# Token numbers written behind the gate's value, and the rank product moved to other banks and later steps

## The chip, the core and the metric

The kernel runs on one core of a Trainium2 chip. The metric is the device time in microseconds (us) of one execution. Instructions run on TensorE (PE: matmuls; its weight loads are listed as PEld), VectorE (DVE), ScalarE (ACT) and GpSimd (POOL); SyncE (SP) and POOL issue DMAs. Each engine takes its instructions in the order in which they were queued to it, and an instruction that waits for a semaphore holds up what is queued behind it.

## The reference

Three stages follow each other. A gated delta-rule attention over 4 batches, 8 heads, 768 tokens and a head size of 48, then a dense layer pair, then a layer with 8 experts of which each token takes one:

```python
for t in range(S):
    kt, vt, bt = (k_n[:, :, t], v[:, :, t], beta[:, :, t, None])
    y[:, :, t] = np.einsum('bhd,bhde->bhe', q[:, :, t], state)
    v_old = np.einsum('bhde,bhd->bhe', state, kt)
    state = state + bt[:, :, :, None] * np.einsum('bhd,bhe->bhde', kt, vt - v_old)
...
h = x @ w_in                      # 384 -> 2048
x = np.maximum(0.01 * h, h) @ w_out
...
e_idx = np.argmax(x @ w_gate, axis=1)          # one of 8 experts
out[mask] = gate_w[mask, None] * eom[mask, e, None] * (np.maximum(x[mask] @ w1[e], 0.0) @ w2[e])
```

## The kernel before

**Chunks and steps.** The 768 positions are cut into 12 chunks of 64 (`NCH`); with the 4 batches a chunk is 256 tokens. The function `weave` runs a loop over n from 0 to 95. Chunk p = n // 8 is in its attention while n runs over its eight steps s = n % 8 (generator `chain`), and beside it run the dense layer of the chunk before (`moe1_up`, `moe1_down`, a sixteenth of its width in two halves at each step) and the tail of the chunk before that (`moe1_tail`, `gate`, `place`). For each pair of chunks the generator `prepare` makes key grams (`k_gram`), norms and the inverse of a 32x32 triangular matrix (`inverse`), which for all pairs but the first is a row of 60 small operations on POOL (L207 and L209) that ends with L211. `back` converts the expert weights (L476 on ACT, L477 on DVE) in the gaps.

**The tail of a chunk.** `moe1_tail` reads the dense layer's result from PSUM into two tiles `row` of 128 tokens, 386 words wide: 384 words of values (L535 on ACT, L536 on DVE), then at word 384 the gate's value (L627) and at word 385 the token number (L628, a constant plus an offset; it needs nothing but the buffer). Three steps later the gate product runs (`gate`, at s = 4), and two steps after that `place` runs (s = 6): five matmuls make `rk`, the rank of each token among those of its expert (L604 to L608), DVE turns it into positions `pi` (L619 to L625), and POOL scatters both row tiles into the DRAM table `xd` by an indirect DMA each (L630). A row tile's buffer is used again two chunks later, so a chunk's first write into it waits until the scatter of the chunk two before has been read out.

**What sets the order.** On PE the order from n = 16 on is the order in which the program is written (a manual schedule). On DVE, ACT, POOL and SP a scheduler places each instruction by its own model of when inputs and buffers are ready, unless `issue_after` ties it to another one. PSUM banks come from pools: `psL` (2 banks; `h` of `moe1_up`, the gate product, and `rk`), `psS` (2 banks; key grams `ga`, query grams `gq`, the outputs `y`), `psA` (2 banks; `ks` of the chain), `psO`.

**Lines that the steps touch.** L317 on DVE writes the start value of a chunk's `ks`; L325 on PE adds the old state's product to it and is the chunk's first matmul of the chain; L295 splits `ks` into `r` and `u` for the matmuls L302. L493 is `moe1_up`'s matmul, L498 to L501 make its activation, L512 is `moe1_down`'s matmul. L260 to L262 mask and split the query gram. L164 is the first POOL operation of a pair's norms, L218 turns the inverse for the chain.

Of the kernel before, what the change touches and what calls it, by code (L numbers as in the profile page):

```python
# [8 lines left out]
F32 = mybir.dt.float32  # L9
# [3 lines left out]
ALU = mybir.AluOpType  # L13
# [5 lines left out]
CH = 64  # L19
NCH = S // CH  # L20
# [494 lines left out]
def flip_pe(k, dst, src, engines, n):  # L515
    for h in range(2):
        tp = k.psS.tile([128, 3, 128], F32, tag="psS", name=f"tp{h}_{n}")
        for kk in range(3):
            q = 3 * h + kk
            k.nc.tensor.matmul(tp[:, kk], src[:, 128 * q : 128 * q + 128], k.ident, start=True, stop=True)  # L520
        d = dst[:, 3 * h : 3 * h + 3]
        if engines[h] is k.nc.scalar:
            engines[h].activation(d, tp, AF.Copy)
        else:
            engines[h].tensor_copy(d, tp)


def moe1_tail(k, c, o):
    nc = k.nc
    V, A, G, PE = nc.vector, nc.scalar, nc.gpsimd, nc.tensor  # L530
    row, rv = [], []
    for t in range(2):
        row.append((k.m2 if c >= NCH - 2 else k.p2).tile([128, XCOL], I32, tag="row" if c >= NCH - 2 else f"row{c % 2}", name=f"row{t}{c}"))
        rv.append(row[t][:, 0:384].bitcast(F16))
        A.activation(rv[t][:, 0:384], o[t], AF.Copy, scale=2.0**-14)  # L535
        V.scalar_tensor_tensor(rv[t][:, 384:768], o[t], 2.0**-14, rv[t][:, 0:384], op0=ALU.mult, op1=ALU.subtract)  # L536
    xT2 = [k.m2.tile([128, 6, 128], F16, tag="x2t", name=f"x2t{t}{c}") for t in range(2)]
    if c < NCH - 2:
        for t in range(2):
            nc.sync.dma_start_transpose(out=xT2[t], in_=rv[t])  # L540
        yield
        yield
        yield
    else:
        yield
        for t in range(2):
            flip_pe(k, xT2[t], rv[t], (A, A), f"{t}{c}")
            yield
    lg_ps = k.psL.tile([128, 2, 16], F32, tag="psL", name=f"lgp{c}")
    for t in range(2):  # L550
        n = 0
        for kk in range(3):
            for l, r in PASSES:
                PE.matmul(lg_ps[:, t], xT2[t][:, 3 * l + kk], k.wg[r][:, kk], start=(n == 0), stop=(n == 8))
                n += 1
    fin = gate(k, c, lg_ps, row)
    yield
    if c < NCH - 2:
        yield
    fin()  # L560
    yield


def gate(k, c, lg_ps, row):
    nc = k.nc
    V, A, G, PE = nc.vector, nc.scalar, nc.gpsimd, nc.tensor

    def small(n, shape, dt=F32):
        return k.m1.tile(shape, dt, tag=f"g_{n}", name=f"g_{n}{c}")

    def bc(ap, n=8):
        return ap.unsqueeze(2).to_broadcast([128, 2, n])

    lg = small("lg", [128, 2, 16])
    V.tensor_scalar(lg, lg_ps, 2.0**-18, None, op0=ALU.mult)
    mx = small("mx", [128, 2])
    V.tensor_reduce(mx, lg[:, :, 0:8], axis=AX.X, op=ALU.max)
    ls = small("ls", [128, 2, 8])
    V.tensor_tensor(ls, lg[:, :, 0:8], bc(mx), op=ALU.subtract)
    ex = small("ex", [128, 2, 8])  # L580
    A.activation(ex, ls, AF.Exp)
    s = small("s", [128, 2])
    V.tensor_reduce(s, ex, axis=AX.X, op=ALU.add)
    eq = small("eq", [128, 2, 8])
    i8 = k.iota8.unsqueeze(1).to_broadcast([128, 2, 8])
    V.scalar_tensor_tensor(eq, ls, 0.0, i8, op0=ALU.is_ge, op1=ALU.mult)
    ix = small("ix", [128, 2])
    V.tensor_reduce(ix, eq, axis=AX.X, op=ALU.min)
    oh = small("oh", [128, 2, 8])
    V.tensor_tensor(oh, i8, bc(ix), op=ALU.is_equal)  # L590
    ohh = small("ohh", [128, 2, 8], F16)
    V.tensor_copy(ohh, oh)
    return lambda: place(k, c, row, lg, s, oh, ohh)


def place(k, c, row, lg, s, oh, ohh):
    nc = k.nc
    V, A, G, PE = nc.vector, nc.scalar, nc.gpsimd, nc.tensor

    def small(n, shape, dt=F32):  # L600
        return k.m1.tile(shape, dt, tag=f"g_{n}", name=f"g_{n}{c}")

    rk = k.psL.tile([128, 3, 8], F32, tag="psL", name=f"rk{c}")
    PE.matmul(rk[:, 0], k.tri, ohh[:, 0], start=True, stop=True)  # L604
    PE.matmul(rk[:, 1], k.tri, ohh[:, 1], start=True, stop=False)
    PE.matmul(rk[:, 1], k.ones, ohh[:, 0], start=False, stop=True)
    PE.matmul(rk[:, 2], k.ones, ohh[:, 0], start=True, stop=False)
    PE.matmul(rk[:, 2], k.ones, ohh[:, 1], start=False, stop=True)  # L608
    ol = small("ol", [128, 2, 8])
    og = small("og", [128, 2])  # L610
    V.tensor_tensor(ol, oh, lg[:, :, 8:16], op=ALU.mult)
    V.tensor_reduce(og, ol, axis=AX.X, op=ALU.add)
    z = small("z", [128, 2])
    A.activation(z, og, AF.Exp, scale=-1.0)
    V.tensor_scalar(z, z, 1.0, None, op0=ALU.add)
    V.scalar_tensor_tensor(z, s, 1e-9, z, op0=ALU.add, op1=ALU.mult)
    V.reciprocal(z, z)
    pos = small("pos", [128, 2, 8])
    V.tensor_tensor(pos, rk[:, 0:2], k.run.unsqueeze(1).to_broadcast([128, 2, 8]), op=ALU.add)  # L619
    V.tensor_tensor(k.run, rk[:, 2], k.run, op=ALU.add)  # L620
    V.tensor_tensor(pos, pos, oh, op=ALU.mult)
    ps = small("ps", [128, 2])
    V.tensor_reduce(ps, pos, axis=AX.X, op=ALU.add)
    pi = k.m2.tile([128, 2], I32, tag="pi", name=f"pi{c}")
    V.tensor_copy(pi, ps)  # L625
    for t in range(2):
        V.tensor_scalar(row[t][:, 384:385].bitcast(F32), z[:, t : t + 1], 2.0**-27, None, op0=ALU.mult)  # L627
        V.tensor_scalar(row[t][:, 385:386], k.tid[:, t : t + 1], float(CH * c), None, op0=ALU.add)  # L628
    for t in range(2):
        nc.gpsimd.indirect_dma_start(  # L630
            out=k.xd[:, :], out_offset=bass.IndirectOffsetOnAxis(ap=pi[:, t : t + 1], axis=0), in_=row[t][:, :], in_offset=None
        )
# [260 lines left out]
def weave(k):  # L893
# [130 lines left out]
    for n in range(8 * NCH):  # L1024
# [42 lines left out]
        if down is not None:  # L1067
            moe1_down(k, *down)
            if down[1] == 7:
                tail = moe1_tail(k, down[0], k.o)  # L1070
# [27 lines left out]
def finish(k, up, tail):  # L1098
    ts = None
    for s in range(9):  # L1100
        down, up = up, None
        if s < 8:
            moe1_up(k, NCH - 1, s)
            up = (NCH - 1, s, k.gg)
        if s == 0:
            ts = [gather(k, i, k.ridx0) for i in range(4)]
        if tail is not None:
            next(tail, None)
        moe1_down(k, *down)
        if down[1] == 7:  # L1110
            tail = moe1_tail(k, down[0], k.o)
    next(tail)
    moe2_up(k, ts[0])
    next(tail)
    next(tail)
    moe2_up(k, ts[1])
    next(tail)
    moe2_down(k, ts[0])
    next(tail)
    moe2_up(k, ts[2])  # L1120
    moe2_down(k, ts[1])
    moe2_up(k, ts[3])
    moe2_down(k, ts[2])
    moe2_tables(k)
    ahead = {s: gather(k, s, k.ridx) for s in range(4)}
    moe2_down(k, ts[3])
    return ahead
# [121 lines left out]
```

## Time and profile before

| what | value |
|---|---|
| median of 3 runs | 967.54 us (966.23 to 970.23) |
| profiled execution, own time | 970.8 us |
| its span | 969.1 us |
| PE busy | 778.9 us, 80% of the span |
| PEld busy | 599.7 us, 62% |
| DVE busy | 588.6 us, 61% |
| ACT busy | 405.0 us, 42% |
| POOL busy | 348.6 us, 36% |
| mean granted TensorE clock | 0.948 of full speed |

The table is an average over stages. From 0 to about 200 us the attention starts and weights are converted; from 200 to about 610 us the weave runs with `prepare` beside it; from there to 745 us it runs without it; then come the experts. A time in brackets at the end of a trace row is how long the engine stood idle before that row, followed by what ended it.

### The profile page before, as it was taken

How to read it: one execution, taken by the hardware profiler on the slowest of the kernel's cores; microseconds unless marked ns; L12 is line 12 of the kernel's file. 1: busy time of each engine (PE TensorE's matmuls, PEld its weight loads, DVE VectorE, ACT ScalarE, POOL GpSimd, SP SyncE). 2: the span in 40 equal slices, each digit the busy share in tenths (PEclk: the TensorE clock that was granted, in tenths of full speed). 3: DMA queues.
4: the chain of work that ended last, by engine and by line, in shares of the span. 5: the costliest groups of instructions: out<-in, count | busy, mean ns of one | idle time of the engine just before them, and what ended most of it. 6: DMA issues, size and time to landing. Idle time of an engine off the chain costs nothing. (4 is left out here: it accounts for less than half of the span.)

```text
span 969.1 us, 36443 instructions
## 1 busy us (share of the span) xinstructions
PE 778.9 (80%) x15996; PEld 599.7 (62%) x15996; DVE 588.6 (61%) x1304; ACT 405.0 (42%) x788; POOL 348.6 (36%) x526
## 2 busy tenths in 40 slices
PE   3033796858978698768978688999989889999994
PEld 3023565646756476646756466777767778877782
DVE  6999995747868577766958468686546222222221
ACT  5247655534664356634564245555332111111110
POOL 0027993684028810585028800000202322122210
PEclk9999997988999799998999789999999999999998
DMA  8425332435544455544554344555681743899460
GB/s 267 150 81 175 131 111 61 131 103 157 163 129 139 142 162 157 131 134 138 162 146 126 103 109 148 137 155 127 257 353 37 232 84 76 197 317 300 104 172 11
DMA packets 100965, 145.67 MB, mean 150 GB/s; under 512 B 43120, under 2 KB 70547, under 8 KB 97986
## 3 DMA queue, kind: packets, MB, share of 16 engines
q1 hardware_dynamic: 95682, 128.29, 44.9%
q0 software_dynamic: 5120, 15.00, 4.8%
q8 instruction: 127, 2.08, 0.9%
q14 instruction: 36, 0.29, 0.1%
HBM read 152.28 MB, written 35.42 MB: 194 GB/s over the span
## 5 line engine op out<-in xcount | busy, mean ns | idle before, releaser
L493 PE MATMUL h<-xx,win 128*128 128x256 f16 x1728 | 223.4, 287 | 4.8 <-issue 3.2
L493 PEld LDWEIGHTS <-win 128*128 128x128 f16 x1728 | 172.0, 103 | 37.5 <-issue 5.0
L512 PE MATMUL o<-wout,gh 128*128 128x384 f16 x768 | 188.0, 330 | 2.2 <-ACT gh L500 0.9
L835 PEld LDWEIGHTS <-wb 128*128 128x128 f16 x2016 | 118.5, 99 | 10.7 <-issue 4.2
L512 PE MATMUL o<-wout,gl 128*128 128x384 f16 x384 | 124.2, 329 | 0.0
L500 ACT ACTIVATE gh<-h 128x512 f16<-128x512 f32 x96 | 57.3, 597 | 159.5 <-DVE h L499 159.5
L630 POOL DMA_INDIRECT xd<-row,pi x24 | 25.3, 1055 | 261.2 <-issue 139.2
L839 DVE SCALAR_TENSOR_TENSOR h<-hp,h 128x512 f16<-128x512 f32 x48 | 33.2, 691 | 126.0 <-ACT h L838 126.0
L835 PE MATMUL hp<-xT,wb 128*128 128x128 f16 x1728 | 103.5, 223 | 5.0 <-DMA xT<-row 2.5
L512 PEld LDWEIGHTS <-gh 128*128 128x128 f16 x768 | 73.8, 99 | 44.7 <-issue 3.7
L838 ACT ACTIVATE h<-hp 128x512 f16<-128x512 f32 x48 | 28.7, 597 | 166.1 <-PE hp L835 166.1
L849 PE MATMUL o<-wb,h 128*128 128x384 f16 x576 | 97.4, 326 | 0.0
L501 DVE TENSOR_TENSOR gl<-h,gh 128x512 f16<-128x512 f32 x96 | 66.3, 690 | 46.0 <-ACT gh L500 45.9
L209 POOL TENSOR_TENSOR x<-x,tmp 128x30 f32<-128x30 f32 (+9 forms) x150 | 86.0, 573 | 11.1
L499 DVE SCALAR_TENSOR_TENSOR h<-h,g 128x512 f32<-128x512 f32 x96 | 66.4, 691 | 37.6 <-ACT g L498 37.5
L207 POOL TENSOR_TENSOR tmp<-x 128x30 f32<-128x30 f32 (+9 forms) x150 | 84.8, 565 | 10.8
L498 ACT ACTIVATE g<-h 128x512 f32<-128x512 f32 x96 | 57.4, 598 | 69.5 <-PE h L493 64.9
L853 POOL DMA_INDIRECT out_dram<-y,row x24 | 23.9, 998 | 150.0 <-DVE y L852 133.8
L849 PEld LDWEIGHTS <-h 128*128 128x128 f16 x576 | 55.3, 98 | 34.3
L477 DVE SCALAR_TENSOR_TENSOR whl<-we,whl 128x512 f16<-128x512 f32 x96 | 73.7, 779 | 0.0
L302 PE MATMUL ks<-r,z 32*32 32x48 f16 x2304 | 27.2, 189 | 44.0 <-ACT z L235 27.1
L476 ACT ACTIVATE whl<-we 128x512 f16<-128x512 f32 x96 | 57.9, 623 | 0.1
(250 smaller groups left out, 1132.5 us busy)
## 6 DMA issues: line engine op xcount, KB each, us to landing
wb<-wd SPq DMA_DIRECT2D x56, 1536.0 KB
we<-in_we_dram SPq DMA_DIRECT2D x96, 256.0 KB
wd<-whl SPq DMA_DIRECT2D x96, 256.0 KB
kt<-in_kt_dram SPq DMA_DIRECT2D x22, 224.0 KB
qt<-in_qt_dram SPq DMA_DIRECT2D x22, 224.0 KB
nv<-in_kv_dram SPq DMA_DIRECT2D x12, 384.0 KB
kn<-in_kv_dram SPq DMA_DIRECT2D x12, 384.0 KB
w<-in_win_dram SPq DMA_DIRECT2D x6, 512.0 KB
```

The lines of the kernel that those rows point to most:

```text
L207: E.tensor_tensor(tv, x[:, q, j : j + 1].to_broadcast([128, n, j]), x[:, j : j + 1, 0:j].to_broadcast([128, n, j]), op=ALU.mult)
L209: k.after = E.tensor_tensor(x[:, q, 0:j], x[:, q, 0:j], tv, op=ALU.add)
L476: nc.scalar.activation(hl[:, 0], w32, AF.Copy, scale=sc)
L477: nc.vector.scalar_tensor_tensor(hl[:, 1], w32, sc, hl[:, 0], op0=ALU.mult, op1=ALU.subtract)
L493: PE.matmul(hp[:, ff], k.win[l][:, f, kk], xx[:, r, kk], start=(n == 0), stop=(n == 8))
L498: A.activation(g32, hp, AF.Copy, scale=0.01 * 2.0**-10)
L499: V.scalar_tensor_tensor(hp, hp, 2.0**-10, g32, op0=ALU.mult, op1=ALU.max)
L500: k.mark = A.activation(gh, hp, AF.Copy)
L501: k.mark_gl = V.tensor_tensor(gl, hp, gh, op=ALU.subtract)
L512: k.mark_down = k.nc.tensor.matmul(k.o[t], gg[l][:, ff, 128 * t : 128 * t + 128], k.wout[r][:, f], start=(f == 0 and i == 0), stop=(f == N ...
L835: PE.matmul(hp[:, ff], w1[:, l, kk, 128 * f : 128 * f + 128], t.xT[:, 3 * r + kk], start=(i == 0), stop=(i == 8))
L849: nc.tensor.matmul(o, t.h[l][:, f], w2[:, r, f], start=(i == 0), stop=(i == 23))
```

## The change

The write of the token number (L628, now L631) is tied by `issue_after` to the write of the gate's value into the same row tile. `rk` comes from the banks of `psS` instead of `psL` for chunks 0 to 9. And for chunks 0 to 8 the loop in the tail pauses three times instead of once, so that `place` runs four steps after the gate instead of two: at s = 0 of the next chunk instead of s = 6.

```diff
@@ moe1_tail
     if c < NCH - 2:
-        yield
+        for _ in range(3 if c < NCH - 3 else 1):
+            yield
     fin()
@@ place
-    rk = k.psL.tile([128, 3, 8], F32, tag="psL", name=f"rk{c}")
+    ps = (k.psS, "psS") if c < NCH - 2 else (k.psL, "psL")
+    rk = ps[0].tile([128, 3, 8], F32, tag=ps[1], name=f"rk{c}")
...
-        V.tensor_scalar(row[t][:, 384:385].bitcast(F32), z[:, t : t + 1], 2.0**-27, None, op0=ALU.mult)
-        V.tensor_scalar(row[t][:, 385:386], k.tid[:, t : t + 1], float(CH * c), None, op0=ALU.add)
+        last = V.tensor_scalar(row[t][:, 384:385].bitcast(F32), z[:, t : t + 1], 2.0**-27, None, op0=ALU.mult)
+        with k.tc.issue_after(last.ins):
+            V.tensor_scalar(row[t][:, 385:386], k.tid[:, t : t + 1], float(CH * c), None, op0=ALU.add)
```

DVE before, at the start of chunk 3 (n = 24). `row02` is the row tile of chunk 2's first 128 tokens; its buffer is that of `row00`, chunk 0's:

```order
L260 TENSOR_TENSOR gq3_1_4387<-gq3_1_4387,amask_119 128x512
L628 TENSOR_SCALAR row02_6373<-crow_528 128x1
L262 TENSOR_TENSOR ap3_4300<-gq3_0_4386,ap3_4300 128x512
L262 TENSOR_TENSOR ap3_4300<-gq3_1_4387,ap3_4300 128x512
L317 SCALAR_TENSOR_TENSOR ks03_4547<-nv3_2064,nw1_907 128x384
L317 SCALAR_TENSOR_TENSOR ks13_4548<-nv3_2064,nw1_907 128x384
```

The same place of DVE now, up to the positions of chunk 0 (`pi0`):

```order
L260 TENSOR_TENSOR gq3_1_4358<-gq3_1_4358,amask_119 128x512
L262 TENSOR_TENSOR ap3_4300<-gq3_0_4357,ap3_4300 128x512
L262 TENSOR_TENSOR ap3_4300<-gq3_1_4358,ap3_4300 128x512
L317 SCALAR_TENSOR_TENSOR ks03_4518<-nv3_2064,nw1_907 128x384
...
L295 SCALAR_TENSOR_TENSOR r3_4515<-ks13_4519,r3_4515 128x384
L621 TENSOR_TENSOR g_pos0_4702<-rk0_4687,run_530 128x16
L622 TENSOR_TENSOR run_530<-rk0_4687,run_530 128x8
L623 TENSOR_TENSOR g_pos0_4702<-g_pos0_4702,g_oh0_4128 128x16
L499 SCALAR_TENSOR_TENSOR h2_0_4661<-h2_0_4661,g322_0_4680 128x512
L625 TENSOR_REDUCE g_ps0_4706<-g_pos0_4702 128x2
L627 CAST pi0_4708<-g_ps0_4706 128x2
```

The early write into chunk 2's row tile is gone from between L260 and L262, and the five small operations on chunk 0's ranks, which stood ahead of L260, now stand behind L317 and L295.

POOL at the end of a pair's inverse (L211; L164 is the first operation of the next pair), the difference between the two, with the scatters of chunk 0 (`row00`, `row10`) and chunk 1:

```order
 L209 TENSOR_TENSOR x2_3523<-x2_3523,tmp2_3699 128x30
 L211 TENSOR_TENSOR x2_3523<-x2_3523,nz2_3527 128x1024
-L630 DMA xd_57<-row01_4868,pi1_5696 24577x386
-L630 DMA xd_57<-row11_4871,pi1_5696 24577x386
+L633 DMA xd_57<-row00_3496,pi0_4708 24577x386
+L633 DMA xd_57<-row10_3499,pi0_4708 24577x386
+L633 DMA xd_57<-row01_4868,pi1_6111 24577x386
+L633 DMA xd_57<-row11_4871,pi1_6111 24577x386
 L164 TENSOR_TENSOR nz3_6404<-ny3_6403 128x32
```

Chunk 0's two scatters, which stood inside the inverse, have moved behind it; chunk 1's stay where they were. The same holds for chunks 2 and 3, 4 and 5, 6 and 7.

## Rows read from the trace of the kernel before

**Rows 1.** Busy time by stretch: length, then PE, PEld, DVE, ACT, POOL, clock, DMA.

```profile
200.00:610.00 410.00, 333.13 (x8188) 249.73 (x8187) 283.10 (x579) 207.01 (x413) 181.71 (x303) 0.91 0.48 138
```

**Rows 2.** Waits from 200 to 610 us: us in total, times, longest.

```profile
PE ks L325 <- DVE ks L317: 46.1, 16, 11.2
PE rk L604 <- DVE gl L501: 6.2, 4, 2.2
...
DVE row L628 <- DMA xd<-row,pi: 44.7, 8, 11.5
```

**Rows 3.** Timeline of DVE, start of chunk 3: start, length, line.

```profile
218.62 0.15 DVE L628 TENSOR_SCALAR row<-crow 128x1 int32<-128x1 f32 x1 [11.52 <-DMA xd<-row,pi]
...
219.89 1.59 DVE L317 SCALAR_TENSOR_TENSOR ks<-nv,nw 128x384 f32<-128x384 f32 x2
...
225.35 1.01 DVE L295 SCALAR_TENSOR_TENSOR r<-ks,r 128x384 f16<-128x384 f32 x2
...
227.40 0.70 DVE L499 SCALAR_TENSOR_TENSOR h<-h,g 128x512 f32<-128x512 f32 x1 [1.04 <-ACT g L498]
```

**Rows 4.** Timeline of POOL, end of the same pair's inverse.

```profile
215.65 1.19 POOL L630 DMA_INDIRECT xd<-row,pi  x1 [0.24 <-issue]
...
228.95 1.91 POOL L211 TENSOR_TENSOR x<-x,nz 128x1024 f32<-128x1024 f32 x1
```

**Rows 5.** Timeline of PE, start of chunk 3.

```profile
220.73 0.20 PE L325 MATMUL ks<-sc,kc 48*64 48x48 f16 x1 [11.16 <-DVE ks L317]
221.53 1.48 PE L325 MATMUL ks<-sc,kc 48*64 48x48 f16 x95 [0.61 <-DVE ks L317]
222.95 3.73 PE L493 MATMUL h<-xx,win 128*128 128x256 f16 x18
```

**Rows 6.** Timeline of DVE and PE, starts of chunks 5, 7 and 9.

```profile
327.29 0.15 DVE L628 TENSOR_SCALAR row<-crow 128x1 int32<-128x1 f32 x1 [8.06 <-DMA xd<-row,pi]
...
437.83 0.15 DVE L628 TENSOR_SCALAR row<-crow 128x1 int32<-128x1 f32 x1 [9.69 <-DMA xd<-row,pi]
...
547.57 0.15 DVE L628 TENSOR_SCALAR row<-crow 128x1 int32<-128x1 f32 x1 [9.76 <-DMA xd<-row,pi]
...
549.65 0.19 PE L325 MATMUL ks<-sc,kc 48*64 48x48 f16 x1 [7.74 <-DVE ks L317]
```

**Rows 7.** Timeline of DVE and PE, start of chunk 4.

```profile
267.46 0.15 DVE L628 TENSOR_SCALAR row<-crow 128x1 int32<-128x1 f32 x1 [1.27 <-DMA xd<-row,pi]
...
268.14 0.18 PE L325 MATMUL ks<-sc,kc 48*64 48x48 f16 x1 [0.93 <-DVE ks L317]
268.61 1.01 PE L325 MATMUL ks<-sc,kc 48*64 48x48 f16 x95 [0.29 <-DVE ks L317]
269.55 2.14 PE L493 MATMUL h<-xx,win 128*128 128x256 f16 x18
```

**Rows 8.** Busy time by stretch behind the first long wait, columns as above.

```profile
220.70:226.50 5.80, 5.16 (x114) 4.08 (x114) 4.84 (x7) 2.82 (x5) 5.17 (x9) 0.52 0.56 161
```

**Rows 9.** Timeline of DVE and POOL, scatters of chunk 1 and next norms.

```profile
262.89 0.15 DVE L625 CAST pi<-g_ps 128x2 int32<-128x2 f32 x1
...
268.19 1.19 POOL L630 DMA_INDIRECT xd<-row,pi  x1 [3.39 <-DMA xd<-row,pi]
...
276.98 0.68 DVE L499 SCALAR_TENSOR_TENSOR h<-h,g 128x512 f32<-128x512 f32 x1
...
286.03 0.23 POOL L164 TENSOR_TENSOR nz<-ny 128x32 f32<-128x32 f32 x1 [16.65 <-DVE ny L162]
```

**Rows 10.** Timeline of DVE and ACT, next users of inverse and row.

```profile
257.74 1.24 DVE L218 STREAM_TRANSPOSE zt<-x 128x1024 f32<-128x1024 f32 x1
...
278.71 0.86 ACT L535 ACTIVATE row<-o 128x384 f16<-128x384 f32 x2
```

**Rows 11.** Timeline of DVE, two L477 beside L211, and two without.

```profile
229.79 2.22 DVE L477 SCALAR_TENSOR_TENSOR whl<-we,whl 128x512 f16<-128x512 f32 x2
...
342.61 1.28 DVE L477 SCALAR_TENSOR_TENSOR whl<-we,whl 128x512 f16<-128x512 f32 x2
```

## The prediction

> **What bounds the kernel now.** I read the busy table by stretch first. From 200 to 610 us PE is busy for 333.13 of 410 us and DVE for 283.10 [rows 1]: no engine is full, PE is nearest, so what makes PE wait there is worth reading. The waits of that stretch, longest in total first, then show one line far ahead of all others. PE stood 46.1 us before L325 for DVE's L317, and 6.2 us before L604; DVE itself stood 44.7 us, in 8 places, before L628 for a scatter to be read out [rows 2]. The timelines show that these are one thing. At the start of chunk 3 DVE has everything for L262 and L317, but L628 stands ahead of them and waits 11.52 us [rows 3]. L628 writes a constant into the row tile of chunk 2, into which L535 writes its first values only at 278.71 [rows 10]; it needs the buffer of chunk 0, whose scatter POOL issues at 215.65, in between the operations of an inverse that ends at 230.86 [rows 4]. L317 follows at 219.89, and PE, out of work until then, starts L325 at 220.73 after 11.16 us [rows 5]. The starts of chunks 5, 7 and 9 show the same, with 8.06, 9.69 and 9.76 us [rows 6]; those of chunks 4, 6, 8 and 10 show it small, 1.27 us at the first of the four [rows 7].
>
> **Part 1, the token number behind the gate's value.** The write itself is kept, 0.15 us on DVE, and is now where the buffer has long been this chunk's own, since L535 and L536 have written to it. Nothing waits there. What goes is the stall, and I ask at each place what is late next. Chunk 3: without L628, L262 starts 11.5 us earlier, and so does L317, which is 2.1 us ahead of PE's L325 by the distance of 218.62 and 220.73; PE then meets its data at 209.2 to 209.6, when it is ready. All of its 11.16 us go. Chunks 5 and 7: DVE gains 8.06 and 9.69. Chunk 9: PE stood only 7.74 us [rows 6], since it came later than DVE; 7.74 go. Together 11.16 + 8.06 + 9.69 + 7.74 = 36.65 us. Small places: DVE's waits leave 44.7 - (11.52 + 8.06 + 9.69 + 9.76) = 5.67 us for the four, 1.42 each; PE stood 0.93 before L325 at the one shown [rows 7]. So 0.93 to 1.42 at each, 3.7 to 5.7 us in all; I take the middle, 4.7.
>
> **The clock behind a stall.** Behind the 11.16 us the granted clock is 0.52 for 5.8 us, the lower of its two levels (1.2 of 2.4 GHz) [rows 8]: the 95 matmuls of L325 take 1.48 us and the 18 of L493 3.73 [rows 5], where chunk 4's start shows 1.01 and 2.14 [rows 7]. That is 0.47 + 1.59 = 2.06 us, and 8.2 us if the three other long stalls cost as much. The Trainium skill (TensorE: Matmul & The Clock Gate, HAM oscillation) says that idle gaps throttle PE again, so that the matmuls behind each run cold; rows 8 agree, and by that rule alone the whole 8.2 would come back. I take half, 4.1, because DVE is late next there: L295, which feeds PE's next matmuls of the chain, ends at 226.36, 7.7 us after L628 [rows 3], and this stretch of DVE's queue does not shorten with PE's clock. Bounds 0 and 8.2.
>
> **Part 2, the rank product in other banks and two steps later.** The five matmuls and five small DVE operations stay; they move. In psL, `rk` took a bank that L501 had still to read, and four times PE waited, 6.2 us in all [rows 2]. In psS the banks of the query grams have been read by L262 ahead of L317, so at the new place, behind L493 of the next chunk's first step, nothing has to be waited for. The 6.2 us don't all come back: `moe1_down`, a few matmuls behind, needs the same L501. Bounds 0 and 6.2; I take half, 3.1. On DVE the first three small operations now stand between L295 and L499. At chunk 3's start L499 stood 1.04 us for ACT [rows 3], which covers them; at chunk 4's start L499 has no wait before it at 276.98 [rows 9], so there they can cost their own time, some 0.5 us if each takes what L628 and L625 take, 0.15 us [rows 3, 9]. Four such places, 2 us at most; I take 0, as PE has the whole of `moe1_down` before it needs L499's result.
>
> **Part 3, what the later positions do to POOL.** The scatters of the even chunks leave the inverse and stand behind it. The inverse gets shorter by them (1.19 us for the one shown [rows 4]). Two users could be late. The first is the row tile's next writer, L535, at 278.71 [rows 10], some 13 us earlier now, near 265; chunk 0's two scatters would start near 228, when the inverse ends. The one issued at 215.65 was read out by 218.62, 3.0 us later [rows 3, 4]; two behind each other make 6 us, 10 with some delay, so 238. Cover: 265 - 238, some 27 us. The second is the inverse's user L218 at 257.74 [rows 10], near 244 now, against an end near 228: 16 us of cover. The odd chunks' scatters are tighter. Before, `pi` was cast at 262.89 and the second scatter ended at 269.38, 6.5 us later; L164, held by DVE, started at 286.03 [rows 9]. Now the cast stands behind the L499 that ran at 276.98, so near 278.0, the second scatter ends near 284.5, and 1.5 us of cover are left. If the scatter takes 4 us longer, POOL is 2.5 us late at each of three pairs, and DVE's norms behind it, 7.5 us in all. I take 0.
>
> **The sum.** 36.65 + 4.7 + 4.1 + 3.1 = 48.6 us off the profiled execution's own 970.8 us (its span of 969.1 and 1.7 around it) gives 922.2. That execution stands 3.3 us above the median of 967.54; against the median the same gain gives 919.0, which I forecast. Gains at their upper bounds: 36.65 + 5.7 + 8.2 + 6.2 = 56.8, so 910.8. At their lower bounds, 36.65 + 3.7 = 40.4, less 2 and 7.5 of costs, 30.9 are left, so 936.7.
>
> **Rivals.**
>
> *POOL and DVE get in each other's way, 930.* The 39 us in which DVE stood were time in which POOL had the tiles to itself. Beside POOL's L211 two L477 took 2.22 us, without it 1.28 [rows 4, 11]. If the three long operations of each of four inverses now each meet a DVE that has no slack, that is 12 x 0.94 = 11.3 us, so 930.3. Against it: such meetings exist before too, and move rather than multiply. The Trainium skill (SBUF — State Buffer, Who interferes with whom) says that a DVE instruction with two SBUF inputs and a POOL one that reads SBUF lock each other out whole. L477 has two such inputs, and the rows agree in direction: 2.22 against 1.28 is a delay of half of L211's 1.91, not of all of it; by the rule in full it would be 12 x 1.91 = 22.9 us, so 942.
>
> *The wait moves on to DVE, 943.* If DVE's queue behind the stall had been what PE would meet next everywhere, half of the gain is given back within the chunk: 967.5 - 24.3 = 943.2. Against it: DVE's 283.10 us in a stretch of 361 would be 78%, PE's 333.13 would be 92%, so PE is still nearer to full.
>
> *The change doesn't reach the stall, 967.5.* It would need an early write to stay ahead of L317. The order of DVE's instructions shows none, so this has little chance.
>
> *Slower.* L535 takes L628's part: it waits for the same scatter, now behind the whole inverse, and holds ACT's queue, with DVE's L536 behind it. It decides from 27 us on: if the scatters land more than that later than I reckon, each of the seven chunks that use a row buffer again waits for the rest. To eat 48.6 us, each has to be late by 27 + 7 us. At 10 us beyond the cover the time is 967.5 - 48.6 + 70 = 989. Against it: the 27 us count from the end of the inverse, behind which POOL's queue holds nothing but the scatters and L164.
>
> **Chances.** The forecast (909 to 926) 0.72, POOL and DVE in each other's way (926 to 936) 0.14, the wait on DVE 0.07, no change 0.04, slower 0.03. The range 909 to 934 takes in the first and most of the second, about 0.83. A measurement of this kernel can tell about 0.5%, 5 us, from no change: faster 0.93, the same 0.04, slower 0.03.
>
> **What would show it.** In the profile after: no wait of DVE for a scatter between 200 and 610 us, and PE before L325 under 1 us at each chunk's start; the clock at its upper level behind it; L493 near 2.1 us there; the starts of chunks 3 and 5 some 96.5 us apart (108.67 before, by 218.62 and 327.29 [rows 3, 6], less a quarter of 48.6). PE before the rank product: nothing. POOL's L164 still released by DVE; if by a scatter, part 3 was wrong. A wait of ACT's L535 for a scatter would make the whole prediction wrong, and so would PE waiting as long for L295 or L499 as it did for L317.

## The result and the profile after

The changed kernel took 918.89 us (median of 4 executions, 910.93 to 920.65) beside 968.88 us for the kernel before: a ratio of 0.9463, 95% interval 0.9432 to 0.9495. The forecast was 919.0. In a second comparison, beside its variants, the ratio was 0.9518 (0.9495 to 0.9541), 924.46 against 971.97 us; there the gain is 4.8% and not 5.4%. Both lie in the forecast's range when they are put on its base of 967.54 us: 915.6 and 920.9. That the total came so near is partly luck, as the terms below show.

The profiled execution took 919.24 us (span 917.4), 51.6 us less than the 970.8 of before. The same stretch of the kernel now runs from 200 to about 566 us. Its busy times, in the columns of [rows 1]:

```profile
200.00:566.00 366.00, 330.17 (x8228) 246.49 (x8227) 291.27 (x585) 210.15 (x419) 189.62 (x302) 0.96 0.56 157
```

PE is busy for 330 of 366 us, 90% against 81% before. The granted clock is 0.96 of full speed against 0.91. DVE's busy time in this stretch rose from 283 to 291 us.

PE's waits there (us in total, times, longest), which answer to [rows 2]. No line of DVE waits for `xd<-row,pi` any more; its longest wait for anything but ACT is now 2.0 us:

```profile
PE ks L302 <- issue: 9.8, 5, 2.6
PE ks L325 <- DVE ks L317: 6.4, 10, 1.5
PE rk L606 <- DVE lx L142: 5.6, 2, 3.1
PE ks L325 <- issue: 4.2, 1, 4.2
```

The 46.1 us before L325 have become 6.4. The 6.2 us before the rank product have become 5.6 with another name: not L501, the reader of `psL`'s banks, but L142, a reader of key grams in `psS`. The two rows that end in "issue" stand for gaps in the middle of a run of equal matmuls, for which the profile shows no releaser.

The start of chunk 3 on DVE and then on PE (start, length; in brackets the idle time ahead), against [rows 3, 5]:

```profile
204.74 1.29 DVE L262 TENSOR_TENSOR ap<-gq,ap 128x512 f16<-128x512 f32 x2
205.95 1.50 DVE L317 SCALAR_TENSOR_TENSOR ks<-nv,nw 128x384 f32<-128x384 f32 x2
```

```profile
206.58 0.18 PE L325 MATMUL ks<-sc,kc 48*64 48x48 f16 x1 [0.20 <-DVE ks L317]
207.50 0.95 PE L325 MATMUL ks<-sc,kc 48*64 48x48 f16 x95 [0.74 <-DVE ks L317]
208.38 2.14 PE L493 MATMUL h<-xx,win 128*128 128x256 f16 x18
210.36 0.17 PE L606 MATMUL rk<-g_ohh,cmat 128*128 128x8 f16 x1
```

L317 follows L262 with nothing between. PE waits 0.20 us where it waited 11.16, and behind it the 18 matmuls of L493 take 2.14 us instead of 3.73. The rank product of chunk 0 stands behind them, without a wait.

At the start of chunk 4 it is otherwise, and this is what the prediction missed:

```profile
260.37 0.17 PE L606 MATMUL rk<-g_ohh,cmat 128*128 128x8 f16 x1 [2.54 <-DVE lx L142]
263.61 0.97 PE L104 MATMUL ga<-kc 48*64 48x64 f16 x95 [0.86 <-DVE run L622]
```

With chunk 4 `prepare` begins the next pair. Its key grams `ga` have just been put into both banks of `psS`. The rank product has to wait until L142 has read one of them, and the next key gram then waits for L622, the rank product's own reader. Chunk 8 shows 3.06 us in the same place. At chunk 6 key grams lie in both banks too, but there the rank product comes behind a gap of 4.22 us in PE's work and has nothing left to wait for.

POOL at that place, the scatters of chunk 1 and the norms of the next pair, against [rows 9]:

```profile
265.26 0.96 POOL L633 DMA_INDIRECT xd<-row,pi  x1 [30.33 <-ACT gh L500]
268.65 0.96 POOL L633 DMA_INDIRECT xd<-row,pi  x1 [2.43 <-DMA xd<-row,pi]
273.43 0.23 POOL L164 TENSOR_TENSOR nz<-ny 128x32 f32<-128x32 f32 x1 [3.82 <-DVE ny L162]
```

The second scatter ends at 269.61, and POOL then idles for 3.82 us until DVE has its input: the norms are still released by DVE.

### The profile page after: what moved, and what is told of

Read it like the earlier page. It is cut to its first block, busy times and chain, and to the rows that moved or that the text cites. A ratio compares the mean times of both kernels' runs of the same rounds, so it can differ in the third digit from the quotient of the medians.

```text
span 917.4 us, 36446 instructions
## 1 busy us (share of the span) xinstructions
PE 768.7 (84%) x15996; PEld 590.7 (64%) x15996; DVE 592.6 (65%) x1304; ACT 405.2 (44%) x788; POOL 356.6 (39%) x526
## 3 DMA queue, kind: packets, MB, share of 16 engines
q1 hardware_dynamic: 95682, 128.29, 47.4%
## 5 line engine op out<-in xcount | busy, mean ns | idle before, releaser
L493 PE MATMUL h<-xx,win 128*128 128x256 f16 x1728 | 218.6, 284 | 3.3 <-issue 1.7
L493 PEld LDWEIGHTS <-win 128*128 128x128 f16 x1728 | 169.6, 101 | 33.2 <-issue 3.6
L512 PE MATMUL o<-wout,gh 128*128 128x384 f16 x768 | 188.2, 330 | 3.2 <-DVE row L536 1.8
L512 PE MATMUL o<-wout,gl 128*128 128x384 f16 x384 | 124.4, 329 | 0.4 <-DVE gl L501 0.2
L838 PEld LDWEIGHTS <-wb 128*128 128x128 f16 x2016 | 116.5, 98 | 11.4 <-issue 7.8
L838 PE MATMUL hp<-xT,wb 128*128 128x128 f16 x1728 | 101.5, 220 | 5.8 <-DMA xT<-row 5.8
L512 PEld LDWEIGHTS <-gh 128*128 128x128 f16 x768 | 73.1, 99 | 45.5 <-issue 4.5
L501 DVE TENSOR_TENSOR gl<-h,gh 128x512 f16<-128x512 f32 x96 | 66.3, 690 | 44.8 <-ACT gh L500 44.5
L209 POOL TENSOR_TENSOR x<-x,tmp 128x30 f32<-128x30 f32 (+9 forms) x150 | 90.5, 604 | 11.3
L477 DVE SCALAR_TENSOR_TENSOR whl<-we,whl 128x512 f16<-128x512 f32 x96 | 72.6, 768 | 0.0
L302 PE MATMUL ks<-r,z 32*32 32x48 f16 x2304 | 27.7, 188 | 46.7 <-ACT z L235 27.1
```

The costliest lines, as they stand in the source:

```text
L209: k.after = E.tensor_tensor(x[:, q, 0:j], x[:, q, 0:j], tv, op=ALU.add)
L477: nc.vector.scalar_tensor_tensor(hl[:, 1], w32, sc, hl[:, 0], op0=ALU.mult, op1=ALU.subtract)
L493: PE.matmul(hp[:, ff], k.win[l][:, f, kk], xx[:, r, kk], start=(n == 0), stop=(n == 8))
L501: k.mark_gl = V.tensor_tensor(gl, hp, gh, op=ALU.subtract)
L512: k.mark_down = k.nc.tensor.matmul(k.o[t], gg[l][:, ff, 128 * t : 128 * t + 128], k.wout[r][:, f], start=(f == 0 and i == 0), stop=(f == N ...
L838: PE.matmul(hp[:, ff], w1[:, l, kk, 128 * f : 128 * f + 128], t.xT[:, 3 * r + kk], start=(i == 0), stop=(i == 8))
```

## Experiments

Ten kernels were run in three groups, each group on one chip and beside runs of the kernel before on that chip; a ratio is always to these. A gain in us below is what the ratio takes off the median of before. It can differ from the difference of the two medians: for part 1 alone it is 51.8 us against 48.7, since one of its executions took 911.24 us.

### Each part alone

Part 1 alone, the tie:

```diff
-        V.tensor_scalar(row[t][:, 384:385].bitcast(F32), z[:, t : t + 1], 2.0**-27, None, op0=ALU.mult)
-        V.tensor_scalar(row[t][:, 385:386], k.tid[:, t : t + 1], float(CH * c), None, op0=ALU.add)
+        last = V.tensor_scalar(row[t][:, 384:385].bitcast(F32), z[:, t : t + 1], 2.0**-27, None, op0=ALU.mult)
+        with k.tc.issue_after(last.ins):
+            V.tensor_scalar(row[t][:, 385:386], k.tid[:, t : t + 1], float(CH * c), None, op0=ALU.add)
```

> Part 1 alone: the token number is tied to the gate's value, the rank product keeps its banks and its steps. Theory (the gain is DVE's wait for the scatter ahead of L317): all of the gain but the rank product's share, 36.65 + 4.7 + 4.1 = 45.4 us, so about 922 us, a ratio of 0.953 to before; no wait of DVE for a scatter between 200 and 610 us, PE's 6 us before the rank product as before. Rival (the later positions and the other banks are needed for the gain): half of it at most, 944 us or more.

Measured: 922.5 us against 971.18, a ratio of 0.9467 (0.9423 to 0.9512). PE's waits (200 to 600 us):

```profile
PE rk L604 <- DVE gl L501: 5.3, 4, 2.4
PE ks L325 <- issue: 3.1, 1, 3.1
PE ks L325 <- DVE ks L317: 3.0, 5, 0.7
```

DVE has no wait for a scatter left between 200 and 610 us. The rank product waits as before, and yet the whole gain is there. So the tie alone gives what the two parts give together, as far as these intervals can tell.

Part 2 alone, banks and pauses without the tie:

```diff
+        for _ in range(3 if c < NCH - 3 else 1):
+            yield
...
+    ps = (k.psS, "psS") if c < NCH - 2 else (k.psL, "psL")
+    rk = ps[0].tile([128, 3, 8], F32, tag=ps[1], name=f"rk{c}")
```

> Part 2 alone: other banks and three pauses, the token number free. Its write now stands behind L317 and behind L536 of the chunk in progress, but still waits for the scatter of the chunk two before, which POOL now issues behind the whole inverse. Theory: DVE reaches the write near 217 us at chunk 3 and the scatter that is issued near 230 is read out near 233, so DVE waits some 16 us in each odd chunk and some 4 us in each even one, with L295 behind it: 4 x 20 = 80 us on top of the changed kernel's 919, less what PE has left to do without DVE there, 975 to 1000 us. Rival (the write only has to leave its place ahead of L317, the later steps do that as well): 919 to 930 us.

Measured: 968.37 us, ratio 0.9975 (0.9954 to 0.9996): the gain is gone. It had been expected to be slower than before, and it isn't. DVE's wait and PE's, both from 200 to 610 us, then DVE and PE in chunk 3:

```profile
DVE row L630 <- DMA xd<-row,pi: 54.9, 8, 13.4
```

```profile
PE ks L302 <- DVE u L295: 37.0, 10, 11.7
PE o L512 <- ACT gh L500: 10.8, 2, 10.6
```

```profile
231.64 0.15 DVE L630 TENSOR_SCALAR row<-crow 128x1 int32<-128x1 f32 x1 [12.76 <-DMA xd<-row,pi]
```

```profile
232.31 0.19 PE L302 MATMUL ks<-u,lx 32*32 32x48 f16 x1 [11.74 <-DVE u L295]
```

The write of the token number has left the place ahead of L317 and waits further on, for the same scatter, which is now issued behind the inverse. What is queued behind it is L295, and PE stands before L302 instead of L325 (at chunk 7 before L512). The expectation had put the wait at 16 us in odd chunks and 4 in even ones; it is 12 to 13.4 and 0.2 to 1.3. Its mechanism holds and its size was too large: DVE waits 10.2 us more than before in all, and PE's two waits make 47.8 us where it stood 46.1 before L325. The rival, that leaving the place is enough, falls.

### The wait or the place

More row buffers, with the write left free, first four pairs and then one for each chunk:

```diff
-tag="row" if c >= NCH - 2 else f"row{c % 2}"
+tag="row" if c >= NCH - 2 else f"row{c % 4}"
```

> The kernel before with four instead of two pairs of row buffers: a row tile's buffer comes back after four chunks. The token number is written as early as before, ahead of L317, but into a buffer that was read out two chunks ago. Theory: it is the wait that costs, not the place; 45.4 us are gained, 922 us, and DVE's waits for a scatter are under 1 us together. Rival (the place in DVE's order, or POOL beside DVE, costs the time): within 10 us of 967.

Measured: 956.57 us, ratio 0.9853 (0.9826 to 0.988). Neither of the two expected outcomes came. DVE's wait in all, then one of its rows:

```profile
DVE row L628 <- DMA xd<-row,pi: 33.5, 6, 11.6
```

```profile
218.49 0.15 DVE L628 TENSOR_SCALAR row<-crow 128x1 int32<-128x1 f32 x1 [11.57 <-DMA xd<-row,pi]
```

The wait at chunk 3 is as long as before. With twice the buffers, the order puts a write that needs nothing else twice as many chunks ahead: what stands here is now chunk 4's write, and it needs the buffer of the same chunk 0. Only the last long wait and the last small one are gone, since there are no further chunks to be written ahead. So this did not tell wait from place. It is a dose, though: 11.2 us less of DVE's wait went with 14.3 us less of time.

```diff
-tag="row" if c >= NCH - 2 else f"row{c % 2}"
+tag="row" if c >= NCH - 2 else f"row{c}"
```

> The kernel before with a pair of row buffers for each chunk, so that no row tile waits for a scatter. No tie; the order of PE and POOL is that of before, and of DVE's instructions the eight early writes move to the front, near 17 us, where their buffers are free. Theory (the wait is the cost, the tie only one way to be rid of it): the gain of part 1, 921 to 927 us, and no wait of DVE for a scatter. Rival (the tie helps by what else it orders, or POOL beside a DVE without slack costs time): 935 us or more.

Measured: 920.72 us against 972.05, ratio 0.9489 (0.9457 to 0.952). No wait of DVE for a scatter is left between 200 and 600 us; PE's are those of the tie alone:

```profile
PE rk L604 <- DVE gl L501: 5.4, 5, 1.7
...
PE ks L325 <- DVE ks L317: 1.5, 3, 0.9
```

PE's, ACT's, POOL's and SP's order is that of before, and on DVE nothing moved but eight token numbers, to the program's front. The gain is that of the tie, so nothing else that the tie does is needed for it. The writes have left their place ahead of L317 here too; but part 2 alone left that place as well, kept the wait, and gained 0.3%. The two together show that it is the wait that cost the time, and not the place.

### Long waits and small ones

The tie for even chunks alone (whose writes wait long), and for odd ones alone:

```diff
+        with k.tc.issue_after(last.ins) if c % 2 == 0 else ExitStack():
```

> The kernel before with the tie for even chunks only: the writes that wait 8 to 11.5 us at the starts of chunks 3, 5, 7 and 9 are tied, those at the starts of chunks 4, 6, 8 and 10 stay free. Theory: the long stalls and the clock behind them are the gain, 36.65 + 4.1 us, so 927 us; the free writes wait 1.4 us each as before. Rival (POOL issues the scatters late against a faster DVE, so the free writes take over the wait): 5 to 10 us of wait at each of the four, 945 to 960 us.

Measured: 930.35 us against 971.18, ratio 0.9575 (0.9547 to 0.9603): 41.3 us less. DVE's free writes wait 1.7 us at most:

```profile
DVE row L629 <- DMA xd<-row,pi: 6.0, 4, 1.7
```

> The kernel before with the tie for odd chunks only: the four small waits, 1.4 us each at the starts of chunks 4, 6, 8 and 10, go and the four long ones stay. Theory (the waits add up): with 41 us gained by the even chunks and 48 by all, 4 to 7 us are left for these, 964 to 967 us against 971 for the kernel before on this chip; DVE's long waits stay at 8 to 12 us. Rival (the long waits grow by what the small ones gave back, since the scatter they wait for doesn't move): within 2 us of before.

Measured: 964.79 us against 972.05, ratio 0.9929 (0.9901 to 0.9957): 6.9 us less (4.2 to 9.6).

```profile
DVE row L629 <- DMA xd<-row,pi: 41.4, 4, 12.9
```

The long waits are 41.4 us where they were 39.03, so a little of the gain does go into them, but not all: the rival falls. The two halves, 41.3 and 6.9, make 48.2; both together made 0.0533 x 971.18 = 51.8 (47.4 to 56.0). They add up within the intervals.

### What part 2 does

The changed kernel itself, once more beside three variants.

> The changed kernel once more, beside its variants on one chip. Theory (part 2 gives nothing that can be measured): its ratio to before is 0.946 to 0.950, as that of part 1 alone. Rival (part 2 is worth the 3 us and more that were forecast for it): 0.940 to 0.944.

Measured: 924.46 us, ratio 0.9518 (0.9495 to 0.9541). It is above both ranges that had been written down, so it bears out neither; it speaks against the rival, since nothing of 3 us shows on the good side of part 1 alone, 0.9467 (0.9423 to 0.9512).

The rank product left in `psL`, at the later step:

```diff
-    ps = (k.psS, "psS") if c < NCH - 2 else (k.psL, "psL")
+    ps = (k.psL, "psL")
```

> The changed kernel with the rank product left in psL; the tie and the three pauses stay. Theory: the two waits of 2.5 to 3.1 us for L142 go, since psL's banks never hold key grams, and waits for L501 of 1 to 2.4 us come back at up to nine places; PE stands 6 to 10 us before the rank product against 5.6, so 0 to 5 us slower than the changed kernel. Rival (psS is the part that pays): 6 us or more slower.

Measured: 921.57 us, ratio 0.9492 (0.9473 to 0.9511), not told apart from the changed kernel. The waits for L501 that were expected to come back did not: no wait of PE before the rank product is among its rows. Its longest rows, from 200 to 600 us:

```profile
PE ks L302 <- issue: 11.5, 14, 2.0
PE ks L325 <- DVE ks L317: 6.9, 10, 1.6
PE ks L325 <- issue: 2.5, 1, 2.5
```

So the later step alone takes the rank product's wait away, in the old banks, and the rival, that `psS` is the part that pays, falls. But the time isn't below that of part 1 alone: beside it, 5.3 us before the rank product are gone, the wait for L317 has grown from 3.0 to 6.9, and the gaps without a releaser before L302 from 9.2 to 11.5.

The rank product in `psS`, at the old step:

```diff
-        for _ in range(3 if c < NCH - 3 else 1):
+        for _ in range(1):
             yield
```

> The changed kernel with one pause as before; the tie and psS stay. The rank product stands at s = 6 again, POOL's scatters of the even chunks inside the inverse. Theory: at s = 6 psS holds no key grams, PE waits there under 1 us each and 3 us in all, and the time is that of the changed kernel or up to 5 us below it; the later steps bring nothing by themselves. Rival (the scatters inside the inverse delay POOL's users, which is what the later steps mend): 5 us or more slower than the changed kernel.

Measured: 932.15 us, ratio 0.9598 (0.9577 to 0.9618), 7.7 us above the changed kernel. The theory falls. The rival had the size right, but PE's waits show another reason:

```profile
PE gq L104 <- DVE run L622: 19.2, 9, 3.6
```

At s = 6 the rank product itself has its bank at once, but the query grams of the next chunk come right behind it and wait for its reader, 9 times. In `psS` the product has to stand behind the query grams, so the new banks need the later steps.

One step earlier for the odd chunks, to get away from the key grams:

```diff
-        for _ in range(3 if c < NCH - 3 else 1):
+        for _ in range((3 if c % 2 == 0 else 2) if c < NCH - 3 else 1):
```

> The changed kernel with two pauses for odd chunks, three for even ones: the rank products that met key grams in psS at the starts of chunks 4 and 8 now stand one step earlier, behind L493 of s = 7. Theory: the 5.6 us before the rank product, the 0.9 us of L104 for L622 and the clock behind them go, 6 to 10 us less than the changed kernel, near 911. Rival (PE gets to the key grams sooner, but they wait for L142 all the same behind ACT's L131): 0 to 2 us less.

Measured: 926.9 us, ratio 0.953 (0.9511 to 0.9549), no better than the changed kernel: the theory falls. Where the rank product waited for the key grams' reader it now waits for that of the query grams:

```profile
PE rk L606 <- DVE ap L262: 9.5, 4, 3.1
```

## Why the prediction was right, step by step

**What bounds the kernel: right.** It was DVE's wait for the scatter. Three different edits that take it away (the tie, a buffer for each chunk, and the changed kernel) give 4.8 to 5.4%; one that moves it on (part 2 alone) gives 0.3%; and three that take away part of it give part of the time: 3.3 us of wait removed went with 6.9 us of time (4.2 to 9.6), 11.2 with 14.3, 38.7 with 41.3, and all 44.7 with 51.8.

**The long stalls and the clock: right in size, but not for the reason given.** Forecast for both 36.65 + 4.1 = 40.75 us; the tie on even chunks alone measures 41.3 (38.6 to 44.0). What the lower clock cost at the four starts can be read from rows. Before, the 95 matmuls of L325 took 1.48 us at each, and the 18 of L493 took 3.73 at chunk 3 [rows 5] and as follows at chunks 5, 7 and 9:

```profile
330.45 4.02 PE L493 MATMUL h<-xx,win 128*128 128x256 f16 x18
...
442.23 3.32 PE L493 MATMUL h<-xx,win 128*128 128x256 f16 x18
...
551.87 3.12 PE L493 MATMUL h<-xx,win 128*128 128x256 f16 x18
```

Now they take 0.95 and 2.14 us at all four. The stretch behind the start of chunk 3, against 0.52 in [rows 8], has a granted clock of 1.00:

```profile
206.50:212.50 6.00, 5.18 (x131) 3.92 (x130) 5.16 (x9) 3.31 (x6) 5.53 (x7) 1.00 0.49 149
```

That is 7.75 us less of PE's busy time, near the upper bound of 8.2 and in line with the rule quoted from the Trainium skill (TensorE: Matmul & The Clock Gate, HAM oscillation). But not all of it shortened the program. The tie on odd chunks still has the long stalls, part 1 alone has not. From the 95 (or 96) matmuls of L325 behind a stall to the next chunk's first L325 the former needs, over the four places, 186.6 us, the latter 182.3, and the kernel with a buffer for each chunk 182.0. So 4.3 to 4.6 us came back, by one trace of each, close to the 4.1 of the forecast. They are spread unevenly: 3.3 to 3.4 us lie behind chunk 5, and behind chunk 3 nothing came back. There the tie on odd chunks and then part 1 alone show:

```profile
221.50 1.48 PE L325 MATMUL ks<-sc,kc 48*64 48x48 f16 x95 [0.61 <-DVE ks L317]
...
267.04 1.11 PE L325 MATMUL ks<-sc,kc 48*64 48x48 f16 x96
```

```profile
208.92 0.96 PE L325 MATMUL ks<-sc,kc 48*64 48x48 f16 x96
...
255.26 1.11 PE L325 MATMUL ks<-sc,kc 48*64 48x48 f16 x96
```

The reason given for half, that DVE's L295 is late next, does not show: in the changed kernel at chunk 3 L295 ends at 212.53 and PE goes on to L302 at 212.53 without a wait, and from 200 to 566 us L302 waits 0.8 us for L295 in all. What took the rest is open. One part is seen behind chunk 3, where a gap without a releaser before L302 is 1.54 us long in part 1 alone and 0.54 with the tie on odd chunks.

L325 over the whole program, before and after (busy us, mean ns, then idle time ahead):

```profile
L325 PE MATMUL ks<-sc,kc 48*64 48x48 f16 x1056 | 16.5, 209 | 47.9 <-DVE ks L317 46.1 <-issue 1.8
```

```profile
L325 PE MATMUL ks<-sc,kc 48*64 48x48 f16 x1056 | 13.5, 191 | 11.5 <-DVE ks L317 6.4 <-issue 5.1
```

PE's idle time ahead of it fell by 36.4 us, less than the 41.35 of long and small places together, because L317 is still up to 1.55 us late at several starts and one gap of 4.22 us, at chunk 6, has no releaser. Behind that gap L493 takes 4.02 us again.

**The small places: too low, if anything.** Forecast 4.7, measured 6.9 (4.2 to 9.6) with the tie on odd chunks alone.

**Part 2: the term that failed.** Forecast 3.1 us, from the premise that the banks of `psS` have been read by the time the rank product comes. That holds at the starts of odd chunks. At the starts of chunks 4 and 8 both banks hold the next pair's key grams, and PE waits 2.54 and 3.06 us there; in all 5.6 against 6.2. The larger part of the error lies elsewhere: where the wait is really taken away (the later step in `psL`), the kernel is not faster than part 1 alone either, as PE then waits more at L325 for DVE. So no gain from the 6.2 us shows in any run. That they "don't all come back" was in the text, with L501 as the reason; what shows in the traces, one of each kernel, is L317 and the gaps before L302. That the forecast still met the total is luck: part 1 alone measures 51.8 us (47.4 to 56.0) where 45.45 had been forecast for its terms, and this covers what part 2 didn't give. The small places, 6.9 against 4.7, are some of the difference; where the rest comes from isn't shown.

**POOL: right.** The rows of POOL and of DVE at the places that the forecast named:

```profile
228.26 1.91 POOL L211 TENSOR_TENSOR x<-x,nz 128x1024 f32<-128x1024 f32 x1
```

```profile
245.47 1.24 DVE L218 STREAM_TRANSPOSE zt<-x 128x1024 f32<-128x1024 f32 x1
...
264.35 0.17 DVE L627 CAST pi<-g_ps 128x2 int32<-128x2 f32 x1
```

L218 ran 15.3 us behind the end of the inverse, where 16 us of cover had been forecast. The odd chunks' scatters had 3.8 us of cover where 1.5 had been reckoned: the second ended at 269.61, 5.3 us behind the cast, not 6.5. ACT's L535 did not wait for a scatter between 200 and 566 us.

**POOL and DVE in each other's way: the rival had a place, not a price.** DVE's busy time rose by 4.0 us in all, against the 11.3 of the rival, and not at L477 (72.6 us against 73.7) but at L79 (17.8 against 13.5). Three of its ten operations on `q` make the rise, those of chunks 5, 7 and 9, which now run while POOL is in L211. Chunk 5 before, then now with POOL's row first:

```profile
349.58 1.22 DVE L79 SCALAR_TENSOR_TENSOR q<-qt,q 112x1024 f16<-112x1024 f32 x1 [1.26 <-ACT q L78]
```

```profile
326.48 1.91 POOL L211 TENSOR_TENSOR x<-x,nz 128x1024 f32<-128x1024 f32 x1
...
326.86 2.61 DVE L79 SCALAR_TENSOR_TENSOR q<-qt,q 112x1024 f16<-112x1024 f32 x1 [1.26 <-ACT q L78]
```

L211 had 1.53 us to go when L79 began, and L79 took 1.39 us longer; chunks 7 and 9 show 2.67 and 2.72 us. With a buffer for each chunk it was once the other way round: L79 began at 526.56 and took 1.22 us, L211 began at 526.59 and took 2.97 instead of 1.91. So in these rows the one that began second lost nearly all of the time that they shared. The two L477 of [rows 11] fit this: they began 0.84 us into L211, and their delay of 0.94 is most of the 1.07 us that were left. The forecast set it against the whole of L211 and read a half. In part 1 alone L79 takes 13.6 us, so the new meetings come with part 2. Whether they lengthen the program isn't shown.

**The check on the starts was wrong.** From chunk 3 to chunk 5 PE needs 307.90 - 206.58 = 101.3 us, not 96.5: the text gave each pair a quarter of the gain. In this stretch lie the stall of chunk 5, the small one of chunk 4 and the clock behind chunk 3. But behind chunk 3 the clock gave nothing back, the waits of 2.54 and 0.86 us at chunk 4 are new, and so are 1.55 us before L325 at chunk 5, where the forecast had said under 1.

**What stays open.** The gaps without a releaser (15.7 us before L302, L325 and L493 in the changed kernel, 9.8 + 4.2 + 1.7) were not studied. Whether the changed kernel is 2 to 3 us slower than the tie with the rank product in `psL` can't be told: 0.9518 and 0.9492 have intervals that overlap. No variant was clearly better than the changed kernel.

## What to carry to other kernels

An instruction that depends on nothing but a free buffer was put as far ahead here as buffers allowed, and in a queue that runs in order it then made everything behind it wait for the buffer's last reader: look for short instructions with long waits for a DMA, and tie them to a neighbour that comes late anyway. Twice the buffers in the ring gave 14.3 us of 51.8, since the write moved ahead with them; what gave the whole was a buffer that nobody has to give back, or the tie. And a wait that is taken away is not yet a gain: look at what the engine waits for next.

## What had not been expected of the hardware

Single executions of one program lay further apart than the half per cent that was taken as the measure: the changed kernel took 910.93 us once, at a mean granted clock of 0.978, and otherwise 918.55 to 927.87; the tie alone took 911.24 once, at 0.978 too, and otherwise 919.45 to 926.28. The mean clock alone doesn't tell the time, though: two executions of the changed kernel took 921.28 us at 0.917 and 922.16 at 0.969. What differs between them was not looked into.
